# A half-width projection tile doubled to 128 columns, and moved to a bank of its own

## The chip, the cores and the metric

The kernel runs on one core of one Trainium2 chip. The metric is the device time of one launch in microseconds (us), as the median of several runs. The core has five engines, each with an instruction queue of its own that it works off in order: TensorE (PE in the profile, with its weight loads shown apart as PEld), VectorE (DVE), ScalarE (ACT), GpSimd (POOL) and SyncE (SP), which issues the transfers. PE writes to eight banks of PSUM, each with 128 partitions and 2 KB (512 fp32 values) in each partition; DVE and ACT read the banks.

A matmul on PE has a stationary operand, loaded first, of up to 128 rows (the dimension summed over) and up to 128 columns (the partitions of the output), and a moving operand. The profile writes the stationary operand as rows*columns, and then the moving one: `64*128 64x256` is a matmul with 64 rows and 128 columns in use, through which 256 columns of the moving operand pass.

## The reference

Four layers over a sequence of 2048 tokens of width 576, in bf16: attention, gated layer, attention, gated layer, all with a layer norm before and a residual sum after. Both attention layers use the same weights, as do both gated layers.

```python
def _A_ref(x, wqkv, wo):                    # 32 heads of 18, window of 8 with dilation 2
    qkv = (x @ wqkv).reshape(B, S, 3, H, Dh).transpose(2, 0, 3, 1, 4)
    q, k, v = qkv[0], qkv[1], qkv[2]
    ...
    attn = _softmax(logits, axis=-1)
    o = jnp.einsum("bhsw,bhswd->bhsd", attn, vg)
    return o.transpose(0, 2, 1, 3).reshape(B, S, D) @ wo

def _B_ref(x, w_gate, w_up, w_down):        # F = 4608
    h = (x @ w_gate) * (x @ w_up)
    return h @ w_down

x = x + _A_ref(_layernorm(x), wqkv, wo)
x = x + _B_ref(_layernorm(x), w_gate, w_up, w_down)
x = x + _A_ref(_layernorm(x), wqkv, wo)
x = x + _B_ref(_layernorm(x), w_gate, w_up, w_down)
```

## The kernel before

**Stages.** The tokens go through in 18 stages, each an attention part (`attention`) and a gated part (`glu`) over the same tokens of one layer pair. The first four stages have 128 tokens (`nst == 1`, `n = 128`), the other fourteen 256 (`nst == 2`, `n = 256`). While the gated part of one stage runs on PE, the attention part of a following one runs mostly on DVE, ACT and through transfers. Its few PE pieces, the projections among them, are put between the matmuls of the gated part. A planner (`Plan.run`) does that when the kernel is built, from estimated costs; what comes out is a fixed order of instructions on each engine.

**Banks.** The gated part and the projections share four banks, two called `pg` (gate) and two called `pu` (up). One `pg` and one `pu` together are a unit. A unit is given to one piece of work at a time. In the gated part PE fills `pg` and `pu` (L793 for the rows 0 to 511 of the width 576, L804 for the 64 rows left), ACT copies `pg` out (L815), and DVE multiplies `pu` into it (L816, output `h`). L832 and L834 then multiply `h` with the third weight into the banks `acc` and `acct`.

**Projections.** `project` takes two units, `ua` and `ub`, and makes three groups of matmuls, all by the helper `mm` at L469: `full` over the four blocks of 128 rows for the tiles of `ua`; then `tails`, over the last 64 rows, for the tiles of both units; then `full` for the tiles of `ub`. The 64 rows of the tails lie twice in SBUF, on partitions 0 to 63 and 64 to 127, and the list of tails says which half each of them uses. The profile shows two tails that stand next to each other, use different halves and write different banks, at the same time.

**Weights.** q, k and v have 576 columns each, 1728 together. In `wqkv` columns 0 to 511 are q, 512 to 1023 k, 1024 to 1535 v, and then come the remaining 64 of q (1536), of k (1600) and of v (1664). So there are thirteen tiles of 128 columns and a fourteenth of 64. A tile is written (bank, place in the bank, first column, columns), with bank 0 for `pg` and 1 for `pu`, and the place in steps of `n`. An entry of a list of tails is (half, unit, tile), with unit 0 for `ua`.

With 256 tokens there are two calls of `project`: "q" does q and k, 512 columns each, with four tiles in each unit. "v" has the tiles `ut` in `ua`, which are the rest of q with the rest of k, and the rest of v, and the tiles `uv` in `ub`, which are v's 512 columns. In "v" both tiles of `ua` lie in its `pg`, and its `pu` is not used. With 128 tokens there is one call, "a": `ua` has q and k, `ub` has v and `ut`, with `ut` in `pu`.

**Evictions.** `ev_t` (L550 for q, L522 or L520 for k and v) copies the three rests of 64 out of the unit to partitions 0 to 63 of `qT`, `kT` and `vT`. The rest of k comes from partitions 64 to 127 of its bank already before the change.

**Order.** PE, ACT and DVE each go through their fixed order. A piece of PE work that writes a bank waits until the engine that last read that bank is done.

## Time and profile before

| | |
|---|---|
| median of 3 runs | 1088.74 us (1088.43 to 1090.1) |
| profiled execution, first to last instruction (span) | 1085.9 us |
| DVE busy | 756.5 us (70%) |
| ACT busy | 369.4 us (34%) |
| DMA, HBM read and written | 125.11 MB and 10.88 MB |
| projections L469, matmuls into `pg` and into `pu` | 720 and 540 |

The median lies 2.8 us over the span: the span counts from the first to the last instruction, and the run's time takes in what lies around them. In a timeline a row is a stretch of like instructions: start, length, engine, line, operation, output and input, shapes, count, and where the engine had been idle before it, how long and what ended it. A matmul takes longer from start to end than the next one needs to follow it, since they are pipelined, so what a matmul costs is read from start to start.

### The profile page before, as it was taken

The numbers are of one execution on the slowest core, as the hardware profiler recorded it, in microseconds if no ns is written. First come the engines' busy times: TensorE is split into PE (matmuls) and PEld (weight loads), VectorE is DVE, ScalarE is ACT, GpSimd is POOL, SyncE is SP. The second block draws the span as 40 slices with busy tenths as digits, with TensorE's granted clock in tenths as the row PEclk, the third lists the DMA queues.
The fourth block names the chain that finished last, engine by engine and source line by source line (L and its number), as shares of the span: only waits on it lengthen the run. The fifth ranks groups of instructions, "written<-read, shape, count | busy, mean of one in ns | idle before, by whom it ended". The sixth has DMA issues, their size and how long they took to land.

```text
span 1085.9 us, 25407 instructions
## 1 busy us (share of the span) xinstructions
PE 1071.7 (99%) x10797; PEld 788.8 (73%) x10797; DVE 756.5 (70%) x1345; ACT 369.4 (34%) x756; POOL 8.7 (1%) x39
## 2 busy tenths in 40 slices
PE   8999999999999999999999999999999999999998
PEld 6787877777777777777777777777777777777775
DVE  7677987685959876685967769596876869472222
ACT  5544254332421444232133332333243332213121
POOL 3000000000000000000000000000000000000000
PEclk9999999999999999999999999999999999999999
DMA  9963764745253644435363634527263443534331
GB/s 275 343 191 101 208 167 114 183 81 160 78 149 109 145 134 106 114 98 164 104 172 108 150 104 117 136 77 169 83 162 91 116 126 99 156 110 119 97 112 55
DMA packets 155089, 146.16 MB, mean 135 GB/s; under 512 B 43104, under 2 KB 152672, under 8 KB 154976
## 3 DMA queue, kind: packets, MB, share of 16 engines
q1 hardware_dynamic: 154976, 144.55, 49.4%
q8 instruction: 84, 1.38, 0.5%
q14 instruction: 29, 0.24, 0.1%
HBM read 125.11 MB, written 10.88 MB: 125 GB/s over the span
## 4 chain that ended last, share of the span: by engine, by line
PE 95%; DVE 2%; DMA 1%; issue 1%; SPq 0%; ACT 0%; DVEq 0%; ACTq 0%
PE pg L793 24%; PE pu L793 23%; PE acc L832 23%; PE pg L804 7%; PE pg L469 7%; PE pu L469 4%; PE pa L746 4%; PE acct L834 3%; DMA wraw<-in_A_wqkv_dram 1%; DVE h L816 1%; DMA a_dram<-s 0%; SPq L257 0%; DVE prod L714 0%; DMA ab<-a_dram 0%; PE pa L680 0%
## 5 line engine op out<-in xcount | busy, mean ns | idle before, releaser
L816 DVE TENSOR_TENSOR h<-pu,g_sb 128x512 bf16<-128x512 f32 x288 | 196.5, 686 | 204.9 <-ACT g_sb L815 152.5
L815 ACT CAST g_sb<-pg 128x512 bf16<-128x512 f32 x288 | 168.3, 585 | 478.6 <-PE pu L804 393.1
L832 PE MATMUL acc<-wd,h 128*128 128x512 bf16 x1152 | 306.3, 380 | 0.0
L793 PE MATMUL pg<-xnT_B,wg 128*128 128x256 bf16 (+1 forms) x2592 | 300.8, 261 | 0.8 <-ACT xnT_B L431 0.8
L793 PE MATMUL pu<-xnT_B,wu 128*128 128x256 bf16 (+1 forms) x2592 | 299.3, 261 | 0.0
L793 PEld LDWEIGHTS <-wg 128*128 128x128 bf16 x2592 | 212.4, 98 | 61.3 <-issue 26.2
L793 PEld LDWEIGHTS <-wu 128*128 128x128 bf16 x2592 | 230.9, 98 | 23.3
L834 PE MATMUL acct<-wd,h 128*128 128x64 bf16 x1152 | 222.0, 193 | 0.0
L832 PEld LDWEIGHTS <-h 128*128 128x128 bf16 x1152 | 112.7, 98 | 118.0
L714 DVE TENSOR_TENSOR prod<-vT,ab 128x1280 bf16<-128x1280 bf16 (+1 forms) x127 | 93.1, 742 | 63.5 <-DMA ab<-a_dram 63.3
L469 PEld LDWEIGHTS <-wqkv 128*128 128x128 bf16 (+1 forms) x1260 | 97.0, 98 | 36.9 <-issue 18.9
L834 PEld LDWEIGHTS <-h 128*128 128x128 bf16 x1152 | 112.9, 98 | 2.2
L580 DVE TENSOR_TENSOR prod<-qT,kT 128x2560 bf16<-128x2560 bf16 (+1 forms) x72 | 95.6, 1332 | 1.0 <-ACT kT L522 0.4
L469 PE MATMUL pg<-xnT_A,wqkv 128*128 128x256 bf16 (+4 forms) x720 | 91.6, 262 | 1.9 <-issue 0.8
L731 DVE TENSOR_TENSOR oT<-oT,prod 128x1280 bf16<-128x1280 bf16 (+1 forms) x119 | 90.9, 764 | 3.1
L804 PE MATMUL pg<-xnT_B,wgu_t 64*128 64x256 bf16 (+1 forms) x648 | 88.0, 260 | 0.0
L804 PE MATMUL pu<-xnT_B,wgu_t 64*128 64x256 bf16 (+1 forms) x648 | 88.0, 260 | 0.0
L469 PE MATMUL pu<-xnT_A,wqkv 128*128 128x256 bf16 (+5 forms) x540 | 70.9, 261 | 2.7 <-DVE h L816 2.1
L804 PEld LDWEIGHTS <-wgu_t 64*128 64x128 bf16 x1296 | 47.0, 94 | 32.3 <-issue 27.8
L746 PE MATMUL pa<-wo_p,oT 128*128 128x288 bf16 x310 | 48.2, 286 | 0.1
L375 ACT ACTIVATE xn<-xf,nmr,rstd 128x576 bf16<-128x576 f32 x47 | 40.7, 866 | 8.8 <-DVE nmr L367 8.8
L584 DVE TENSOR_TENSOR prod<-prod 128x1024 bf16<-128x1024 bf16 (+1 forms) x64 | 41.1, 643 | 0.8
(117 smaller groups left out, 562.6 us busy)
## 6 DMA issues: line engine op xcount, KB each, us to landing
wd<-in_B_w_down_dram SPq DMA_DIRECT2D x324, 288.0 KB, 3.2
s_dram<-s SPq DMA_DIRECT2D x13, 512.0 KB, 3.7
prod<-s_dram SPq DMA_DIRECT2D x52, 128.0 KB, 2.9
ab<-a_dram SPq DMA_DIRECT2D x52, 128.0 KB, 2.7
wg<-in_B_w_gate_dram SPq DMA_DIRECT2D x6, 768.0 KB, 9.8
wu<-in_B_w_up_dram SPq DMA_DIRECT2D x6, 768.0 KB, 10.2
out_dram<-ob SPq DMA_DIRECT2D x8, 288.0 KB, 2.7
wraw<-in_A_wqkv_dram SPq DMA_DIRECT2D x4, 432.0 KB, 5.3
```

Of the source, the lines that this page charges most:

```text
L469: nc.tensor.matmul(bank(p_, u)[0:m, e * n:(e + 1) * n], lhsT=wqkv[r_, k, c0:c0 + m], rhs=xnT_A[r_, k, 0:n], start=start, stop=stop, skip_g ...
L580: nc.vector.tensor_tensor(late["prod"][p_ % 2][:, :, :, 0:n], q2, k2, op=ALU.mult)
L584: nc.vector.tensor_tensor(prod[:, :, 0:4:2, 0:n], prod[:, :, 0:4:2, 0:n], prod[:, :, 1:4:2, 0:n], op=ALU.add)
L714: nc.vector.tensor_tensor(js(dst), js(vT[:, :, o0:o0 + n]), abw, op=ALU.mult)
L731: op("DVE", 60 + 3 * n, lambda i_=i_: nc.vector.tensor_tensor(oT[:, :, 0:n], oT[:, :, 0:n], late["prod"][i_ % 2][:, 0, :, 0:n], op=ALU.add ...
L746: nc.tensor.matmul(b()[:, 0:HD], lhsT=oT[:, t, i * P:(i + 1) * P], rhs=wo_p[:, t, hh * HD:(hh + 1) * HD], start=(t == 0), stop=(t == KT - 1))
L793: nc.tensor.matmul(pt[:, e * n:(e + 1) * n], lhsT=w_[:, k, ft * P:(ft + 1) * P], rhs=xT[:, k, 0:n], start=(first and k == 0 and e == 0), s ...
L804: nc.tensor.matmul(ps[:, e * n:(e + 1) * n], lhsT=wgu_t[r_, ft * P:(ft + 1) * P], rhs=xT[r_, KF, 0:n], start=(first and e == 0), stop=not ...
L815: op("ACT", 590, lambda: nc.scalar.copy(g_sb[gs][:, 0:ul], pg[use["slot"]][:, 0:ul]), r=[f"wg_{j}_{u}"], w=[f"g{gs}"], prio=0)
L816: op("DVE", 690, lambda: nc.vector.tensor_tensor(hb[hs][:, 0:ul], pu[use["slot"]][:, 0:ul], g_sb[gs][:, 0:ul], op=ALU.mult), r=[f"wu_{j}_{ ...
L832: nc.tensor.matmul(acc[i][:], lhsT=lhs, rhs=wt[:, e % 2, 0:512], start=(ft == 0), stop=(ft == NFT - 1))
L834: nc.tensor.matmul(acct[:, i * TL:(i + 1) * TL], lhsT=lhs, rhs=wt[:, e % 2, 512:D], start=(ft == 0 and i == 0), stop=(ft == NFT - 1), skip ...
```

## The change

The rest of v becomes a tile of 128 columns: it begins at column 1600 instead of 1664, so it takes the 64 columns of k's rest, which are computed a second time and not read, and the 64 of v's. v's rest then stands on partitions 64 to 127 of the output, and the eviction reads it there. With 256 tokens the tile also moves from the second place in `pg` of `ua` to the first place in `pu` of `ua`, and the six tails of "v" are put in another order. With 128 tokens it stays in `pu` of `ub`, and the order stays. The number of matmuls is the same.

```diff
             uv = [(b_, e, 1024 + P * (2 * b_ + e), P) for b_ in range(2) for e in range(2)]
-            ut = [(0, 0, 1536, P), (0, 1, 1664, TL)]
-            tv = [(0, 1, uv[0]), (1, 1, uv[2]), (0, 1, uv[1]), (1, 0, ut[1]), (0, 0, ut[0]), (1, 1, uv[3])]
-            tb = 0
+            ut = [(0, 0, 1536, P), (1, 0, 1600, P)]
+            tv = [(0, 1, uv[0]), (1, 1, uv[2]), (0, 1, uv[1]), (1, 1, uv[3]), (0, 0, ut[0]), (1, 0, ut[1])]
+            tb, vb, vc = 0, 1, 0
         else:
             uq = [(b_, e, 512 * b_ + P * e, P) for b_ in range(2) for e in range(4)]
-            ut = [(1, 0, 1536, P), (1, 1, 1664, TL)]
+            ut = [(1, 0, 1536, P), (1, 1, 1600, P)]
             uv = [(0, e, 1024 + P * e, P) for e in range(4)]
-            tb = 1
+            tb, vb, vc = 1, 1, n
...
-                (390, lambda u, d: cp(d, vT[0:TL, KF, HALO:HALO + n], bank(tb, u)[0:TL, n:2 * n]), [f"v4{z}"], 0)]
+                (390, lambda u, d: cp(d, vT[0:TL, KF, HALO:HALO + n], bank(vb, u)[TL:P, vc:vc + n]), [f"v4{z}"], 0)]
```

## The prediction, made before the changed kernel ran

> **What bounds the kernel now.** I read the page first, then the clock, then what PE waited for.

> ```profile
> PE 1071.7 (99%) x10797; PEld 788.8 (73%) x10797; DVE 756.5 (70%) x1345; ACT 369.4 (34%) x756; POOL 8.7 (1%) x39
> ...
> PE 95%; DVE 2%; DMA 1%; issue 1%; SPq 0%; ACT 0%; DVEq 0%; ACTq 0%
> ```

> ```profile
> core 0: 1085.9 us, clock 0.999
> ```

> ```profile
> PE pu L469 <- DVE h L816: 2.1, 4, 0.8
> ...
> PE pg L469 <- issue: 0.8, 1, 0.8
> PE pg L793 <- ACT xnT_B L431: 0.8, 1, 0.8
> ```

> The first fence has the busy times and the chain that ended last by engine: PE is busy for 99% of the span and holds 95% of the chain. The granted clock is full. The third fence, PE's waits (total, times, longest), has as its largest entry 2.1 us in four waits, in the projections. So a matmul started earlier on PE ends the kernel earlier, unless one of these few waits takes it back. But busy PE is not PE at its rate, so I looked at how closely projection matmuls follow each other. First, which of them the change touches, from the groups by shape:

> ```profile
> L469 PE MATMUL pg<-xnT_A,wqkv 128*64 128x256 bf16 x56 | 8.7, 279 | 0.0
> ...
> L469 PE MATMUL pg<-xnT_A,wqkv 64*64 64x256 bf16 x14 | 4.1, 293 | 0.0
> ```

> That is four full ones and one tail in each of the 14 stages of 256 tokens. Now the timeline of PE in the last stage, first the projection "q", which has only tiles of 128 columns, then "v":

> ```profile
> 882.03 1.04 PE L469 MATMUL pg<-xnT_A,wqkv 128*128 128x256 bf16 x8
> 882.90 1.04 PE L469 MATMUL pu<-xnT_A,wqkv 128*128 128x256 bf16 x8
> 883.87 0.28 PE L469 MATMUL pg<-xnT_A,wqkv 64*128 64x256 bf16 x1
> 883.87 0.28 PE L469 MATMUL pu<-xnT_A,wqkv 64*128 64x256 bf16 x1
> 883.99 0.27 PE L469 MATMUL pg<-xnT_A,wqkv 64*128 64x256 bf16 x1
> ...
> 884.41 0.28 PE L469 MATMUL pg<-xnT_A,wqkv 128*128 128x256 bf16 x1
> ```

> ```profile
> 887.15 1.37 PE L469 MATMUL pg<-xnT_A,wqkv 128*128 128x256 bf16 x9
> 888.24 0.28 PE L469 MATMUL pu<-xnT_A,wqkv 64*128 64x256 bf16 x1
> 888.36 0.70 PE L469 MATMUL pg<-xnT_A,wqkv 64*128 64x256 bf16 x3
> 888.79 0.28 PE L469 MATMUL pu<-xnT_A,wqkv 64*128 64x256 bf16 x1
> 889.00 1.05 PE L469 MATMUL pg<-xnT_A,wqkv 128*128 128x256 bf16 x8
> ```

> In "q" eight full matmuls go from 882.03 to 882.90: 0.87 us, 0.11 each. The next eight, up to the first tail, take 0.97, so going from 128 rows to 64 costs 0.10. The eight tails start in pairs, two at the same instant (883.87), the next pair 0.12 later, and from the first tail to the next full matmul it is 0.54. In "v" eight full matmuls (the ninth of the first row is the first tail, beside the one at 888.24) take 1.09, and the six tails 0.76, though they are fewer than in "q".

> **The change part by part.** *Full matmuls of the fourteenth tile.* With 128 columns these eight are the like of the second eight of "q": 0.97 instead of 1.09, which saves 0.12. That is the price of changing from 128 columns to 64 in the middle.

> *Tails.* Three pairs would alternate halves and the banks `pg` and `pu` exactly as in "q". Four pairs take 0.54 there, and one pair less is one 256-column matmul less, 0.11, so 0.43 instead of 0.76: 0.33 saved. The cause is that the 64-column tail now is entered and left by a switch, and that it stands next to a tail of the same bank, so that it has no partner. Together 0.45 in an undisturbed stage.

> *Where "v" is cut up.* In two of the 14 stages the output projection L746 stands between the full matmuls and the tails, one of them here:

> ```profile
> 230.56 1.16 PE L469 MATMUL pg<-xnT_A,wqkv 128*128 128x256 bf16 x8
> 231.65 0.79 PE L746 MATMUL pa<-wo_p,oT 128*128 128x288 bf16 x5
> ```

> Eight matmuls again take 1.09, with only full-width work behind them, where the first row of "q" takes 0.87. Both the switch into 64 columns and the one out of it go away: 0.22, with the tails 0.55.

> *The stages with a wait.* The four waits of 2.1 us are first tails into `pu` of `ub`. The longest, on DVE and on PE:

> ```profile
> 826.76 0.68 DVE L816 TENSOR_TENSOR h<-pu,g_sb 128x512 bf16<-128x512 f32 x1
> 827.36 0.82 DVE L714 TENSOR_TENSOR prod<-vT,ab 128x1280 bf16<-128x1280 bf16 x1
> 828.09 0.69 DVE L816 TENSOR_TENSOR h<-pu,g_sb 128x512 bf16<-128x512 f32 x1
> ```

> ```profile
> 826.61 1.37 PE L469 MATMUL pg<-xnT_A,wqkv 128*128 128x256 bf16 x9
> 828.83 0.27 PE L469 MATMUL pu<-xnT_A,wqkv 64*128 64x256 bf16 x1 [0.85 <-DVE h L816]
> ...
> 829.49 0.50 PE L469 MATMUL pg<-xnT_A,wqkv 128*128 128x256 bf16 x3
> ```

> The second `h` ends at 828.78, and the wait at 828.83 whatever PE did before it, so the 0.12 is lost there. From then to the next full matmul it is 0.66, and would be 0.43: 0.23 saved.

> *The wait that the change adds.* `pu` of `ua`, so far unused in "v", is now written by the fifth matmul, 0.44 us after "v" starts (four times 0.11). Behind that matmul the whole of PE is queued. In the stage above the first `h` ends at 827.44, 0.83 after the start, so PE would stop for about 0.4 at the fifth matmul; but it stops until 828.83 anyway, so this costs nothing. In the last stage the bank was last read by a copy of k, and even the copy of the other unit, the later one, is over before "v" starts at 887.15:

> ```profile
> 886.37 0.59 ACT L522 CAST kT<-pu 128x512 bf16<-128x512 f32 x1 [0.28 <-PE pu L469]
> ```

> No price is taken for this wait. Its bound is in the rivals.

> *Weight loads.* 90 stationary operands (56 + 14 above, and 20 in the stages of 128 tokens) grow from 64 to 128 columns.

> ```profile
> L469 PEld LDWEIGHTS <-wqkv 64*128 64x128 bf16 x234 | 9.4, 94 | 12.8 <-issue 9.0 <-DVE wqkv L305 1.0 <-ACT wqkv L307 0.4
> L469 PEld LDWEIGHTS <-wqkv 128*64 128x64 bf16 x72 | 6.2, 109 | 3.7 <-issue 2.9
> ```

> A load of 128 columns takes 94 ns here and one of 64 takes 109, so the wider tile is no dearer to load; and the 0.11 spacing in "q" has such loads in it already. The cost is taken as 0. [...]

> *Evictions.* v's rest is read from partitions 64 to 127 of another bank, as k's rest is already. Same size, same place in ACT's order: 0. The instruction orders of DVE, POOL and SP are unchanged, no DMA moves, and ACT's differs only in the bank named.

> *Stages of 128 tokens.* The 72 loads above are 56 for the wide stages, and 16 for four of these. Tails of the fourth of them, at the place of the 64-column one:

> ```profile
> 65.24 0.22 PE L469 MATMUL pu<-xnT_A,wqkv 64*128 64x128 bf16 x1
> 65.30 0.22 PE L469 MATMUL pg<-xnT_A,wqkv 64*128 64x128 bf16 x1
> 65.44 0.24 PE L469 MATMUL pu<-xnT_A,wqkv 64*64 64x128 bf16 x1
> 65.61 1.28 PE L469 MATMUL pg<-xnT_A,wqkv 64*128 64x128 bf16 x18
> ```

> Paired with the one at 65.30, as those before it are, the tail lets the next start 0.06 later, at 65.36 instead of 65.61: 0.25. The switch into and out of the four full ones is the 0.22 of the cut-up stage. So 0.47 in the fourth stage. In the third there is a pause of 0.8 that ends by "issue" between its last tails (the waits above), of which I can't tell whether it moves along: 0.22 to 0.47, taken as 0.35. The first two lie before PE's wait for the first gated part (`xnT_B`, 0.8 above), which DVE and ACT work leads up to: 0 to 0.47 each, taken as 0.

> *Sum.* 14 wide stages: 8 x 0.45 = 3.60; 2 x 0.55 = 1.10; 4 x 0.23 = 0.92; together 5.62. Narrow: 0.47 + 0.35. In all 6.4 us off a span of 1085.9, which makes 1079.5. The runs' median lies 2.8 over the span, so 1088.74 - 6.4 = 1082.3.

> The bounds: nothing from the tails leaves 8 x 0.12 + 2 x 0.22 + 0.22 = 1.6 (1087.1). All four narrow stages in full (5.62 + 4 x 0.47) and no waits for `h` any more (2.1) would be 9.6 (1079.1).

> **The rivals.**
> *A. Only the full matmuls gain.* If the row change, and not the lack of a partner, made the tails slow, they stay at 0.76: 1087.1. For it: entering and leaving 64 rows stays. Against it: "q" has the same row change, and does four pairs in 0.54.

> *B. The new wait eats the gain.* Units come free in order, `ua` before `ub`. In the ten stages without a wait the first tail, 1.09 after the start, finds `ub` free, so the fifth matmul can wait for at most 1.09 - 0.44 = 0.65. Then the first tail comes 0.53 later than now and the tails still give back 0.33, so a stage loses 0.20; ten lose 2.0, the four others gain 0.92 and the narrow ones 0.8. Net 0.3 lost: 1089.0. For it: the first `h` at 827.44. Against it: that stage waits for `ub` anyway, and the copy of k at 886.96 was early.

> *C. Slower: wider loads come out on PE.* If the loads of the 64-column tiles took half of what those of 128 do, 47 of 94 ns, and PE stood still for the other 47 in each of 90 loads, this would cost 90 x 0.047 = 4.2, and if the pauses around the 64-column tile were load time too, nothing would be gained: 1093.0. [...] Against it: the rows of the loads, and the even spacing in "q". [...]

> *D. More than forecast.* The four waits for `h` also vanish, because transfers land earlier relative to PE: 2.1 more, 1080.2. Nothing in the change moves those transfers.

> **How the numbers follow.** Forecast 0.86, A 0.05, B 0.03, C 0.03, D 0.03. A difference of 0.2%, 2.2 us, is about what a measurement of this kernel can tell from no change. Forecast and D lie beyond it: faster 0.89. A and B lie within: same 0.08. C: slower 0.03. The predicted time is 1082.3. The range takes in D and the first two stages gaining in full on its low side, and half of the tails' gain missing (2.4) on its high side, with some room for the medians of three runs, which spread over 1.7 us: 1080.2 to 1085.4.

> **What would show it.** In the timeline of "v", eight full matmuls up to the first tail in 0.97, three pairs of tails starting at the same instants, 0.43 to the next full matmul, and so a start of the sixteen full ones 1.40 after that of "v" instead of 1.85. No group with 64 columns left. PE's waits for `h` still four, some a little longer, and one more at the fifth matmul around 827. The span near 1079.5, with PE's busy time down by as much. I am wrong if PE shows a wait at the fifth matmul in many stages, if the tails don't pair up, or if a wait elsewhere grows by several us.

## The result, and the profile after

| kernel | median | runs | ratio to the kernel before | 95% interval |
|---|---|---|---|---|
| before | 1088.1 us (1086.38 to 1090.1) | 6 | | |
| after | 1081.81 us (1079.86 to 1085.17) | 6 | 0.9943 | 0.9929 to 0.9958 |

The kernel became faster by 0.57%, 6.3 us; 6.4 were forecast. The profiled execution has a span of 1078.1 us. First the page of the kernel after, the engines' busy times and the chain by engine, then its clock:

```profile
PE 1063.8 (99%) x10797; PEld 787.7 (73%) x10797; DVE 755.1 (70%) x1345; ACT 369.4 (34%) x756; POOL 8.8 (1%) x39
...
PE 95%; DMA 2%; DVE 2%; SPq 1%; issue 1%; ACT 0%; DVEq 0%; ACTq 0%
```

```profile
core 0: 1078.1 us, clock 1.000
```

PE has the same 10797 matmuls, and its busy time fell from 1071.7 to 1063.8, by 7.9, as much as the span (7.8). The other engines' busy times moved by 1.4 us at most. So the time came out of PE's busy stretches, not out of its waits. PE is still 95% of the chain.

PE's waits in the kernel after (total in us, times, longest):

```profile
PE pu L469 <- DVE h L816: 2.1, 4, 0.5
...
PE pg L469 <- issue: 0.9, 1, 0.9
PE pg L793 <- ACT xnT_B L431: 0.8, 1, 0.8
```

The waits for `h` still come to 2.1 in four, the longest 0.5 instead of 0.8; the pause by "issue" and the wait for `xnT_B` are where they were. Now the timeline of PE in the last stage's "v", to be read beside the rows at 887.15 before:

```profile
879.65 0.60 PE L469 MATMUL pg<-xnT_A,wqkv 128*128 128x256 bf16 x4
880.09 0.60 PE L469 MATMUL pu<-xnT_A,wqkv 128*128 128x256 bf16 x4
880.62 0.28 PE L469 MATMUL pg<-xnT_A,wqkv 64*128 64x256 bf16 x1
880.62 0.28 PE L469 MATMUL pu<-xnT_A,wqkv 64*128 64x256 bf16 x1
880.74 0.27 PE L469 MATMUL pg<-xnT_A,wqkv 64*128 64x256 bf16 x1
880.74 0.27 PE L469 MATMUL pu<-xnT_A,wqkv 64*128 64x256 bf16 x1
880.85 0.27 PE L469 MATMUL pg<-xnT_A,wqkv 64*128 64x256 bf16 x1
880.85 0.27 PE L469 MATMUL pu<-xnT_A,wqkv 64*128 64x256 bf16 x1
881.05 1.05 PE L469 MATMUL pg<-xnT_A,wqkv 128*128 128x256 bf16 x8
```

From 879.65 to the first tail at 880.62 it is 0.97 (1.09 before), from there to the next full matmul at 881.05 it is 0.43 (0.76 before). The tails start two at a time, three times. In all eight stages that nothing disturbs, the two stretches are 970 and 434 ns, as they were 1087 and 760 in all eight before, to 1 ns (in three of the eight the output projection L746 follows the tails, and its first matmul ends the second stretch). Where the output projection L746 cuts "v" up, in the stage that stood at 230.56 before:

```profile
227.32 0.60 PE L469 MATMUL pg<-xnT_A,wqkv 128*128 128x256 bf16 x4
227.75 0.60 PE L469 MATMUL pu<-xnT_A,wqkv 128*128 128x256 bf16 x4
228.19 0.78 PE L746 MATMUL pa<-wo_p,oT 128*128 128x288 bf16 x5
```

The eight full ones now take 0.87 (1.09 before). Last, the groups of the kernel after by shape, weight loads and the full matmuls into `pg` (busy time, mean ns of one, idle time before them):

```profile
L469 PEld LDWEIGHTS <-wqkv 128*128 128x128 bf16 x1008 | 85.9, 98 | 19.6 <-issue 7.1 <-DVE wqkv L305 0.6 <-ACT wqkv L307 0.3
...
L469 PE MATMUL pg<-xnT_A,wqkv 128*128 128x256 bf16 x392 | 52.4, 273 | 0.0
```

No group with 64 columns is left, and a load of 128 columns takes 98 ns, where one of 64 took 109 before. All loads together (PEld) fell by 1.1 us.

### The profile page after: what moved, and what is told of

The parts are those of the page before. It is cut to its first block, busy times and chain, and to the rows that moved or that the text cites. A ratio compares the mean times of both kernels' runs of the same rounds, so it can differ in the third digit from the quotient of the medians.

```text
span 1078.1 us, 25413 instructions
## 1 busy us (share of the span) xinstructions
PE 1063.8 (99%) x10797; PEld 787.7 (73%) x10797; DVE 755.1 (70%) x1345; ACT 369.4 (34%) x756; POOL 8.8 (1%) x39
## 4 chain that ended last, share of the span: by engine, by line
PE 95%; DMA 2%; DVE 2%; SPq 1%; issue 1%; ACT 0%; DVEq 0%; ACTq 0%
PE pg L793 24%; PE pu L793 23%; PE acc L832 23%; PE pg L804 7%; PE pg L469 5%; PE pu L469 4%; PE pa L746 4%; PE acct L834 3%; DMA wraw<-in_A_wqkv_dram 1%; DMA a_dram<-s 1%; DMA ab<-a_dram 1%; DVE h L816 0%; SPq L257 0%; DVE prod L714 0%; PE pa L680 0%
## 5 line engine op out<-in xcount | busy, mean ns | idle before, releaser
L816 DVE TENSOR_TENSOR h<-pu,g_sb 128x512 bf16<-128x512 f32 x288 | 196.3, 686 | 200.8 <-ACT g_sb L815 149.6
L793 PE MATMUL pg<-xnT_B,wg 128*128 128x256 bf16 (+1 forms) x2592 | 300.8, 261 | 0.8 <-ACT xnT_B L431 0.8
L793 PE MATMUL pu<-xnT_B,wu 128*128 128x256 bf16 (+1 forms) x2592 | 299.3, 261 | 0.0
L793 PEld LDWEIGHTS <-wg 128*128 128x128 bf16 x2592 | 212.5, 98 | 61.2 <-issue 26.2
L793 PEld LDWEIGHTS <-wu 128*128 128x128 bf16 x2592 | 230.9, 98 | 23.3
L714 DVE TENSOR_TENSOR prod<-vT,ab 128x1280 bf16<-128x1280 bf16 (+1 forms) x127 | 92.9, 741 | 66.5 <-DMA ab<-a_dram 66.4
L469 PEld LDWEIGHTS <-wqkv 128*128 128x128 bf16 (+1 forms) x1260 | 95.4, 97 | 30.3 <-issue 16.1
L469 PE MATMUL pg<-xnT_A,wqkv 128*128 128x256 bf16 (+3 forms) x650 | 79.7, 260 | 1.5 <-issue 0.9
L469 PE MATMUL pu<-xnT_A,wqkv 128*128 128x256 bf16 (+3 forms) x610 | 76.5, 262 | 2.6 <-DVE h L816 2.1
L746 PE MATMUL pa<-wo_p,oT 128*128 128x288 bf16 x310 | 48.2, 286 | 0.1
```

The costliest lines, as they stand in the source:

```text
L469: nc.tensor.matmul(bank(p_, u)[0:m, e * n:(e + 1) * n], lhsT=wqkv[r_, k, c0:c0 + m], rhs=xnT_A[r_, k, 0:n], start=start, stop=stop, skip_g ...
L714: nc.vector.tensor_tensor(js(dst), js(vT[:, :, o0:o0 + n]), abw, op=ALU.mult)
L746: nc.tensor.matmul(b()[:, 0:HD], lhsT=oT[:, t, i * P:(i + 1) * P], rhs=wo_p[:, t, hh * HD:(hh + 1) * HD], start=(t == 0), stop=(t == KT - 1))
L793: nc.tensor.matmul(pt[:, e * n:(e + 1) * n], lhsT=w_[:, k, ft * P:(ft + 1) * P], rhs=xT[:, k, 0:n], start=(first and k == 0 and e == 0), s ...
L816: op("DVE", 690, lambda: nc.vector.tensor_tensor(hb[hs][:, 0:ul], pu[use["slot"]][:, 0:ul], g_sb[gs][:, 0:ul], op=ALU.mult), r=[f"wu_{j}_{ ...
```

## The experiments

Each run's ratio is to the kernel before on the same chip. Beside it stands, where it helps, the stretch of the trace from the first matmul of the first 256-token projection to the start of the kernel's last matmul, called the long stretch: 995.6 us before, 989.7 after. It leaves out the start, which varies for other reasons.

### Up bank and order, but 64 columns

The change moves a tile and pairs the tails, and also widens the tile. This does the first without the second, with 256 tokens only.

```diff
-            ut = [(0, 0, 1536, P), (0, 1, 1664, TL)]
-            tv = [(0, 1, uv[0]), (1, 1, uv[2]), (0, 1, uv[1]), (1, 0, ut[1]), (0, 0, ut[0]), (1, 1, uv[3])]
+            ut = [(0, 0, 1536, P), (1, 0, 1664, TL)]
+            tv = [(0, 1, uv[0]), (1, 1, uv[2]), (0, 1, uv[1]), (1, 1, uv[3]), (0, 0, ut[0]), (1, 0, ut[1])]
...
-                (390, lambda u, d: cp(d, vT[0:TL, KF, HALO:HALO + n], bank(tb, u)[0:TL, n:2 * n]), [f"v4{z}"], 0)]
+                (390, lambda u, d: cp(d, vT[0:TL, KF, HALO:HALO + n], bank(vb, u)[0:TL, vc:vc + n]), [f"v4{z}"], 0)]
```

> Only the bank and the order of the tails are changed in the 14 wide stages; the tile keeps its 64 columns, in all stages. Theory 'columns': the cost lies in going between 64 and 128 columns, whatever the bank. Then in the last wide stage eight full matmuls still take 1.09 us up to the first tail; two pairs of tails start together, the third pair does not (the 64-column tail starts 0.20 after its neighbour), and from the first tail to the next full matmul it is about 0.65 (two pairs 0.23, 0.20 into 64 columns, 0.22 out of it), so 1.74 from the start of "v" to the sixteen full ones (1.85 before, 1.40 with the change). The time is then about 1.4 us under before, 0.9987 of it. Rival 'partner': the tails were slow because neighbours shared a bank; then the tails take 0.43 here, 1.52 in all, and the time is about 4.5 us under before, 0.996.

Measured: 0.9981 (0.9968 to 0.9994), 1086.53 us in 12 runs; the long stretch 994.3, which is 1.3 shorter than before. The timeline of PE in the last "v":

```profile
885.42 0.60 PE L469 MATMUL pg<-xnT_A,wqkv 128*128 128x256 bf16 x4
885.95 0.62 PE L469 MATMUL pu<-xnT_A,wqkv 128*64 128x256 bf16 x4
886.51 0.28 PE L469 MATMUL pg<-xnT_A,wqkv 64*128 64x256 bf16 x1
...
886.74 0.27 PE L469 MATMUL pg<-xnT_A,wqkv 64*128 64x256 bf16 x1
886.94 0.29 PE L469 MATMUL pu<-xnT_A,wqkv 64*64 64x256 bf16 x1
887.16 0.28 PE L469 MATMUL pg<-xnT_A,wqkv 128*128 128x256 bf16 x1
```

Four full matmuls into `pg` go to 885.95, 0.53 instead of the 0.44 that the same four take in the kernel after: entering 64 columns costs 0.09, though the bank and the order are now those of the change. Together with the next four it is 1.09, as before. The last tail starts 0.20 after the one that should be its partner, with the other bank and the other half, and the next full matmul 0.22 after that. So the tails take 0.65. Of the 0.45 per stage, 0.11 belongs to bank and order, and 0.34 to the columns: 0.12 in the full matmuls, 0.22 in the tails.

### Only the stages of 256 tokens, and only those of 128

The first keeps the 64-column tile with 128 tokens, the second keeps everything as before with 256. Both diffs are against the kernel after; `vr`, set for each width of stage, is the first partition on which v's rest stands, 0 for 64 columns and 64 (`TL`) for 128.

```diff
             uq = [(b_, e, 512 * b_ + P * e, P) for b_ in range(2) for e in range(4)]
-            ut = [(1, 0, 1536, P), (1, 1, 1600, P)]
+            ut = [(1, 0, 1536, P), (1, 1, 1664, TL)]
...
-                (390, lambda u, d: cp(d, vT[0:TL, KF, HALO:HALO + n], bank(vb, u)[TL:P, vc:vc + n]), [f"v4{z}"], 0)]
+                (390, lambda u, d: cp(d, vT[0:TL, KF, HALO:HALO + n], bank(vb, u)[vr:vr + TL, vc:vc + n]), [f"v4{z}"], 0)]
```

```diff
-            ut = [(0, 0, 1536, P), (1, 0, 1600, P)]
-            tv = [(0, 1, uv[0]), (1, 1, uv[2]), (0, 1, uv[1]), (1, 1, uv[3]), (0, 0, ut[0]), (1, 0, ut[1])]
-            tb, vb, vc = 0, 1, 0
+            ut = [(0, 0, 1536, P), (0, 1, 1664, TL)]
+            tv = [(0, 1, uv[0]), (1, 1, uv[2]), (0, 1, uv[1]), (1, 0, ut[1]), (0, 0, ut[0]), (1, 1, uv[3])]
+            tb, vb, vc, vr = 0, 0, n, 0
...
-                (390, lambda u, d: cp(d, vT[0:TL, KF, HALO:HALO + n], bank(vb, u)[TL:P, vc:vc + n]), [f"v4{z}"], 0)]
+                (390, lambda u, d: cp(d, vT[0:TL, KF, HALO:HALO + n], bank(vb, u)[vr:vr + TL, vc:vc + n]), [f"v4{z}"], 0)]
```

> The change in the 14 stages of 256 tokens alone; the four stages of 128 tokens as before. The sum of the prediction has 5.6 us for these, 0.9948 of before, 1.40 us from the start of "v" to the sixteen full matmuls, and nothing gained up to the first gated part (33.65 us in the trace of before). If the first two stages, taken as 0 in the prediction, are worth the 1.0 us by which the changed kernel reached its first gated part earlier, this kernel reaches it as late as before; if that 1.0 was spread of the transfers at the start, it may reach it at any time within 1 us of both.

> The change in the four stages of 128 tokens alone; the 14 others as before. By the prediction 0.8 us under before (0.9993); if the first two stages count as the changed kernel's trace suggests, 1.9 us (0.9983), with the first gated part reached 1.0 us earlier than before. 1.85 us from the start of "v" to the sixteen full matmuls in the last stage in either case.

Measured: with 256 tokens alone 0.9938 (0.9926 to 0.995), 1081.56 us in 5 runs, the long stretch 5.7 shorter. With 128 tokens alone 1.0007 (0.9998 to 1.0015), 1089.06 us in 12 runs. The wide stages bring the whole gain, and the narrow ones, forecast at 0.8, brought none in these runs. The narrow stages' matmuls did become shorter. PE in the kernel with 128 tokens alone has a pause between the third stage's tails

```profile
43.49 1.21 PE L469 MATMUL pg<-xnT_A,wqkv 64*128 64x128 bf16 x17 [1.26 <-issue]
```

of 1.26, where it is 0.85 in the profiled execution of the kernel after. Something besides the tails varies there. And the long stretch, in which this kernel differs in nothing from the kernel before, is 0.8 longer in this trace: it has one wait for `h` more, in a "q", that the kernel before does not have.

```profile
385.76 1.03 PE L469 MATMUL pu<-xnT_A,wqkv 128*128 128x256 bf16 x8 [0.67 <-DVE h L816]
```

Either the narrow change moves such a conflict later on, or it is chance. The same kernel a second time, below, bears on that.

### One bank for both tiles

With 128 columns, but both tiles of `ua` in `pg`, and their tails last, in the same half. This takes away the write to `pu` of `ua`, so the new wait at the fifth matmul can't occur.

```diff
-            ut = [(0, 0, 1536, P), (1, 0, 1600, P)]
-            tv = [(0, 1, uv[0]), (1, 1, uv[2]), (0, 1, uv[1]), (1, 1, uv[3]), (0, 0, ut[0]), (1, 0, ut[1])]
-            tb, vb, vc = 0, 1, 0
+            ut = [(0, 0, 1536, P), (0, 1, 1600, P)]
+            tv = [(0, 1, uv[0]), (1, 1, uv[2]), (0, 1, uv[1]), (1, 1, uv[3]), (0, 0, ut[0]), (0, 0, ut[1])]
+            tb, vb, vc = 0, 0, n
```

> 128 columns in all stages, but in the wide ones the tile stays in the gate bank of its unit, at its second place, so the up bank is not written there and the wait at the fifth matmul cannot arise. [...] Theory 'columns': 0.97 up to the first tail, 0.54 from there to the next full matmul, 1.51 in all; the wait for h in the four stages ends as late as in the changed kernel; time 1.5 us above the changed kernel (14 x 0.11), 4.9 us under before (0.9955). Rival 'the new wait costs': if the wait at the fifth matmul costs the changed kernel something that the first tail's wait does not hide, the four stages are shorter here by that much, up to 0.4 us each, and the two kernels come out equal.

Measured: 0.9954 (0.9939 to 0.9969), 1083.55 us in 6 runs, the long stretch 3.4 shorter than before. PE in the last "v", the start of it and then the full matmuls behind its tails:

```profile
885.24 1.25 PE L469 MATMUL pg<-xnT_A,wqkv 128*128 128x256 bf16 x9
886.22 0.28 PE L469 MATMUL pu<-xnT_A,wqkv 64*128 64x256 bf16 x1
...
886.75 1.05 PE L469 MATMUL pg<-xnT_A,wqkv 128*128 128x256 bf16 x8
```

885.24 to the first tails is 0.97 again, and from 886.22 to 886.75 it is 0.54 (540 ns in all eight undisturbed stages, to 1 ns), 0.11 more than with pairs: a tail without a partner costs one more matmul of 256 columns. The stages that wait for `h` are not shorter without the fifth matmul's wait: the four together 10.06 us here, 9.18 in the kernel after, 10.24 before. Each has 0.11 more in its tails by design, and the waits for `h` were longer in this execution: 3.5 in five over the whole kernel, the longest 1.2. So this sum by itself neither shows nor rules out a cost of the fifth matmul's wait.

### The same kernel again, and the order of DVE

The first repeats the kernel with 128 tokens alone, for the question left open above. The second asks whether the remaining waits for `h` can be had. They arise where DVE's product of v (L714) stands in front of `h` and waits for its transfer, as in the kernel after on DVE, and on PE beside it:

```profile
818.76 0.82 DVE L714 TENSOR_TENSOR prod<-vT,ab 128x1280 bf16<-128x1280 bf16 x1 [8.24 <-DMA ab<-a_dram]
819.50 0.68 DVE L816 TENSOR_TENSOR h<-pu,g_sb 128x512 bf16<-128x512 f32 x1
820.10 0.81 DVE L714 TENSOR_TENSOR prod<-vT,ab 128x1280 bf16<-128x1280 bf16 x1
820.84 0.68 DVE L816 TENSOR_TENSOR h<-pu,g_sb 128x512 bf16<-128x512 f32 x1
```

```profile
819.67 0.60 PE L469 MATMUL pg<-xnT_A,wqkv 128*128 128x256 bf16 x4
820.24 0.60 PE L469 MATMUL pu<-xnT_A,wqkv 128*128 128x256 bf16 x4
820.77 0.28 PE L469 MATMUL pg<-xnT_A,wqkv 64*128 64x256 bf16 x1
821.57 0.27 PE L469 MATMUL pu<-xnT_A,wqkv 64*128 64x256 bf16 x1 [0.52 <-DVE h L816]
```

So the planner was told, from the kernel after, to place that product later in the stages from the seventh on:

```diff
-                   margin=0 if on_pe or i_ else 800 if j < 6 else 3500)
+                   margin=0 if on_pe or i_ else 800 if j < 6 else 5000)
```

> The kernel with the change in the four stages of 128 tokens alone, once more, because its first measurement (1.0007, interval 0.9998 to 1.0015) left out the 0.8 us that the prediction gave to these stages, while its trace shows them 0.77 us shorter from the first product to the end of the fourth projection, and 1.0 us of new waits for DVE and ACT in one later projection "q". Theory 'chance': that later wait belongs to transfers that land differently in each execution; then this trace has it at another place or not at all, and the two measurements together are between 0.999 and 1.0005. Rival 'tied': the shift by the narrow stages brings that wait about; then the same projection waits for 1.0 us again, and the time is again not under before.

> The changed kernel, and in the planner the first product with v of a stage (L714, the one that waits for the transfer of ab) is planned 1.5 us later from the seventh stage on (margin 5000 instead of 3500). Theory: the waits of PE for h, 2.1 us in four projections of the changed kernel, come from this product standing in front of two h in DVE's order while its transfer is still under way; planned later it stands behind them. Then PE's waits for h fall below 0.5 us in all, and the time is 1.5 to 2 us under the changed kernel, 0.9925 of before. Rival: the plan only moves the conflict, because every later piece of the stage moves too; then the waits for h are again about 2 us, at other places, and the time is that of the changed kernel, 0.9943.

Measured: 128 tokens alone, again, 0.9988 (0.9978 to 0.9998), 1086.74 us in 12 runs; its trace has no wait in that "q" (1.5 us in four for `h`), and its long stretch is 994.9, 0.7 shorter than before. The two runs of this kernel, 1.0007 and 0.9988, have intervals that only touch; their mean, 0.9998, is no change that these runs could tell. So the wait in "q" comes in one execution and not in the next. But it is not the chance of a single one: the repetition of the kernel after, further down, has the same wait in the same "q",

```profile
385.48 1.03 PE L469 MATMUL pu<-xnT_A,wqkv 128*128 128x256 bf16 x8 [0.67 <-DVE h L816]
```

and the kernels with one bank and with the narrow change in the third and fourth stage only have a shorter one there, 0.21 and 0.50. That is four of the eight traces with a narrow change and the old order of DVE, and none of the five without one. Whether the narrow change makes this wait likelier stays open.

The later product gave 0.9961 (0.9948 to 0.9974), 1084.47 us in 8 runs, above all others with the change in full. PE's waits there:

```profile
PE pu L469 <- DVE h L816: 3.7, 8, 0.5
```

Eight waits instead of four. The conflict of `h` and the product moved to other places and did not shrink, so the theory that the margin was too small falls. That it doubled is one trace: the trace with the narrow change in the third and fourth stage only, further down, has 3.0 in seven without this edit. Nor is the time all due to these waits, for this trace also lost 2.1 us at the start, in the way that the next section shows.

### What the narrow stages give back

The kernel after, the one with 256 tokens alone, and the kernel before, unchanged, together on one chip.

> The changed kernel once more, on the same chip as the kernel with the change in the wide stages alone, so that the two differ by the narrow stages only. The prediction gave those 0.8 us; the traces so far show the first product to the end of the fourth projection shorter by 0.7 to 1.2 us with them. If that reaches the end, this kernel is 0.8 us under the other; if the spread of the transfers at the start covers it, the two are within 0.5 us. From the end of the fourth projection to the last matmul the trace should again be about 5.6 us shorter than before (1013.8 us there), as in the first trace of this kernel (1007.9).

> The change in the 14 wide stages alone, once more, beside the changed kernel on one chip. 5.6 us under before, 0.9948. The trace from the end of the fourth projection to the last matmul as in its first one, 1008.1 us, within 1 us.

> The kernel before, for one more trace. If the first two microseconds of difference between the traces up to the end of the fourth projection are chance, this trace differs from the first one of the same kernel (67.4 us there) by about 1 us too; if they belong to the change, by less than 0.3. From there to the last matmul it is 1013.8 us, within 1 us.

Measured: after 0.9947 (0.9934 to 0.9961), 1082.68 us; 256 tokens alone 0.9948 (0.9935 to 0.996), 1082.62; the one run of the kernel before 1087.68. With or without the narrow change it is the same. The traces show one way in which the gain gets lost. This trace of the kernel after needs 19.04 us from the first matmul of L596 to the first gated part (L793), where its first one needed 16.96 and the kernel before 17.22. The windows of PE (us, its busy time and matmuls, granted clock, DMA share, GB/s), of the kernel after in this repetition:

```profile
16.00:18.00 2.00, 1.22 (x63) 1.00 0.80 222
18.00:20.00 2.00, 1.76 (x55) 0.77 1.06 398
20.00:22.00 2.00, 1.22 (x13) 0.50 1.11 339
```

The granted clock fell to a half from 19.1 to 25.9 us, while fillers, transposes and a projection ran. The first two rows of that projection, here and then in the first trace:

```profile
23.56 1.91 PE L469 MATMUL pg<-xnT_A,wqkv 128*128 128x128 bf16 x16
25.27 1.15 PE L469 MATMUL pu<-xnT_A,wqkv 128*128 128x128 bf16 x12
```

```profile
21.95 1.06 PE L469 MATMUL pg<-xnT_A,wqkv 128*128 128x128 bf16 x16
22.85 0.83 PE L469 MATMUL pu<-xnT_A,wqkv 128*128 128x128 bf16 x12
```

Sixteen matmuls take 1.71 from start to start at half clock and 0.90 at full clock. In all 2.1 us are lost, more than the narrow stages save. The traces with one bank and with the later product lost 1.9 and 2.1 in the same way (18.90 and 19.04 us). Why more often with the narrow change? The wait of PE before the first L596, in the kernel before and then the repetition of the kernel after:

```profile
16.43 0.33 PE L596 MATMUL acct<-prod,Esel 128*32 128x64 bf16 x20 [0.39 <-DVE prod L580]
```

```profile
16.35 0.33 PE L596 MATMUL acct<-prod,Esel 128*32 128x64 bf16 x20 [0.66 <-DVE prod L580]
```

The first stage's shorter tails only bring PE earlier to a wait for DVE, behind the same 21 filler matmuls (L759), and the idle time grows from 0.39 to 0.66 us. Over all runs of this study up to here and in the next experiment, a mean clock of 0.997 or less occurred in 19 of 55 runs of kernels with the change in the first stage (the one with more fillers left out), and in 11 of 88 of those without it, the kernel before among them. This is a rough sign: the mean also takes in the time behind the last matmul, where traces show up to 2.2 us of half clock that costs nothing. This was the theory to be tested next: idle time at the start costs clock.

### More fillers, and no change in the first two stages

The first leaves the change as it is and lets the planner put more fillers into PE's idle time at the start (227 of L759 instead of 127; 50 more were expected, 100 came out). Their product is not used. The second makes the narrow change in the third and fourth stage only; its eviction follows with `vr` as above. Beside them the kernel after, a third time.

```diff
-                    self.warm(min(44, int(max(0, t - clock["PE"] - 100) / 100)))
+                    self.warm(min(80, int(max(0, t - clock["PE"] - 100) / 60)))
```

```diff
-            ut = [(1, 0, 1536, P), (1, 1, 1600, P)]
+            ut = [(1, 0, 1536, P), (1, 1, 1664, TL) if j < 2 else (1, 1, 1600, P)]
```

> The changed kernel, with 50 more filler matmuls (L759, which write nothing that is read) in the first microseconds: the planner puts one for each 60 ns that it expects PE to be idle, instead of each 100 ns, and up to 80 in a row instead of 44. Theory 'clock': in the first stage the faster tails leave PE idle for 0.66 us instead of 0.39 before the first sums (L596), and in some executions the granted clock then falls to half for some 5 us, which costs 2 us up to the first gated part (19.0 instead of 17.0 us from the first L596, seen in three of six traces with the change in the narrow stages, in none of five without). With the gaps filled PE's clock stays at 1.00 from 14 to 30 us, the runs' mean clocks are all 0.998 or more, and no run lies over 1.5 us above the fastest; the median is 0.5 to 1 us under the changed kernel's on the same chip. Rival 'chance': the clock falls whatever PE does there; then as many runs as with the changed kernel have a mean clock of 0.997 or less, and the median is the same within 0.3 us.

> The change in the 14 wide stages and in the third and fourth of the narrow ones; the first two stages, whose PE work has gaps, as before the change. Theory 'clock': the idle time before the first L596 is 0.39 us again, so the clock falls no more often than with the wide stages alone (mean clock 0.997 or less in at most one run of five), and 0.5 to 0.8 us from the third and fourth stage come on top of what the wide stages give: 1080.9 to 1081.8, 0.994 of before. Rival 'nothing from the narrow stages': the same median as with the wide stages alone, 1081.6 to 1082.6.

> The changed kernel, as the control for the two others on the same chip. 1081.8 to 1082.7 as before; a mean clock of 0.997 or less in about a third of the runs by the theory 'clock' (in 16 of 49 so far with the change in the narrow stages, in about 8 of 73 without).

Measured on this chip:

| kernel | median | ratio | 95% interval | mean clock at most 0.997 |
|---|---|---|---|---|
| after, with more fillers | 1081.13 us | 0.9932 | 0.9919 to 0.9945 | 0 of 5 runs |
| narrow change in the third and fourth stage only | 1082.18 us | 0.9941 | 0.9929 to 0.9953 | 1 of 5 |
| after | 1084.0 us | 0.9951 | 0.9938 to 0.9965 | 3 of 6 |

The timeline of PE with more fillers, where the wait before the first L596 was:

```profile
13.89 2.13 PE L759 MATMUL pa<-ident 128*128 128x128 bf16 x35
16.11 0.33 PE L596 MATMUL acct<-prod,Esel 128*32 128x64 bf16 x20
```

and its windows:

```profile
16.00:18.00 2.00, 1.65 (x69) 1.00 0.90 326
...
22.00:24.00 2.00, 2.00 (x36) 1.00 1.06 365
```

The wait is filled, PE is busy for 1.65 of the 2 us from 16 on instead of the 1.22 of the repetition above, and the clock holds. It has the lowest median of all kernels here, 0.9932. The order of the three medians is what the theory asks for, but their intervals overlap, and with a chance of 19 in 55, five runs without a fall come up by luck once in 8 times (36/55 to the fifth power is 0.12). The kernel in the middle did not come out as the theory had it, at 1080.9 to 1081.8; 1082.18 is what its rival, that the narrow stages bring nothing, gave. The kernel after lies above the 1081.8 to 1082.7 expected, and the 2.9 us between it and the kernel with fillers are more than the 0.5 to 1 forecast.

Idle time can't be the whole of it either: the first trace of the kernel after had the same waits of PE around the first L596 as the repetition, and kept its clock. And without the narrow change in the first stages the clock can fall too, only earlier; in the repetition with 256 tokens alone:

```profile
14.00:16.00 2.00, 1.95 (x21) 0.63 0.58 107
16.00:18.00 2.00, 2.00 (x52) 0.51 0.84 266
```

There the stretch at half clock is mostly fillers and sums (L596), and from the first L596 to L793 it took 17.15 us, nothing lost. The trace with the narrow change in the third and fourth stage only is such a case too, and its mean clock of 0.997 is the one counted in the table.

The traces say more about which executions lose the clock. In all fourteen the granted clock changes only at whole multiples of 3.41 us from its first rise: the falls inside the kernel last 3.41 or 6.83 us, and the stretch at full clock lasts 1071.785 us in the first trace of the kernel after and 1078.612 in that of the kernel before, 314 and 316 times 3.41333. That rise, where the fillers' spacing goes from 107 to 56 ns, comes between 4.13 and 6.62 us after the first instruction (6.58 and 6.16 in these two), so these periods lie differently over the kernel in each execution. Count each matmul that starts in a period by its moving columns, times the share of the 128 rows and the share of the 128 columns of the stationary operand that it uses. Then the five periods at full clock ahead of a fall inside the kernel hold 2432 to 2976, and every other one at full clock, up to the last 10 us of the kernel, 3008 or more. The five, and two that kept the clock:

| execution | period, us | PE busy, us | columns so counted | granted clock after it |
|---|---|---|---|---|
| after, repetition | 15.68 to 19.10 | 2.09 | 2432 | half for 6.83 us |
| one bank for both tiles | 14.92 to 18.33 | 2.20 | 2624 | half for 6.83 us |
| later product | 16.31 to 19.72 | 2.21 | 2816 | half for 6.83 us |
| 256 tokens alone, repetition | 11.12 to 14.53 | 2.92 | 2848 | half for 3.41 us |
| third and fourth stage only | 11.45 to 14.86 | 2.94 | 2976 | half for 3.41 us |
| before, repetition | 14.98 to 18.39 | 2.40 | 3008 | full |
| after, first trace | 16.82 to 20.24 | 2.21 | 3328 | full |

So it is not idle time as such: PE's busy time doesn't tell these periods apart, the columns so counted do. The first row is 80 sums of L596, each 64 moving columns with 32 of 128 columns in use, which make 1280, and nine fillers of 128, which make 1152. With more fillers no stretch of 3.41 us between 6 and 60 us of that trace, wherever it begins, holds fewer than 3840, so no fall in five runs need not be luck. This count was found in the traces afterwards, and no run was made to test it.

## Why the prediction was right, point by point

**The sum of the wide stages** was forecast at 5.62. In the profiled executions the eight undisturbed stages gave 8 x (1.847 - 1.404) = 3.54, for 3.60; the two that are cut up 2.565 - 2.016 = 0.55 each, as said; and the four that wait went from 10.24 to 9.18 together, 1.06 for 0.92. That is 5.70, and the long stretch became 5.92 shorter. With 256 tokens alone it was 5.68. Over all seven traces that have this part of the change and the old order of DVE (three of the kernel after, two with 256 tokens alone, and the two of the last experiment) the stretch is 990.5 on the mean, against 995.7 in two of the kernel before: 5.2 less. The spread between them (989.7 to 991.8) is of the size of the waits for `h`, which differ by several tenths from one execution to the next.

**Both pieces of it** hold: 0.12 for the full matmuls is the price of the columns, measured apart by the tile in its own bank with 64 columns. Of the tails' 0.33, put down to the switch and to the missing partner together, the bank and order alone give 0.11, which is the partner, and the columns 0.22. The two add up: the kernel with one bank has the columns without the partner, and its tails go from 0.76 to 0.54, again 0.22. Each part can be had alone, the whole 0.45 only with both.

**Rival A**, only the full matmuls gain, falls with the 0.43. Four pairs in "q" were the right measure for three in "v".

**Rival B**, the new wait at the fifth matmul: it is there, but in three stages only, all of which wait for `ub` anyway. In the rows at 819.67 the fifth matmul starts 0.57 after the first instead of 0.44, so 0.13 of wait, and the first tail into `pu` then still waits 0.52 for the second `h`. The other two are 0.04 and 0.28. The eleven other stages have none. In all three the first tail waits 0.52 more behind it, for the other unit, so the fifth matmul's wait lies inside a wait that PE has anyway. The kernel that can't have it had longer waits for `h` in its one trace, and settles nothing here.

**Rival C**, dearer loads, falls with the row of loads: 98 ns for 128 columns. That a load of 64 columns takes half of one of 128, 47 of 94 ns, is shown by no run; it took 109. **Rival D**, the waits for `h` vanish: they stayed at 2.1, and in the attempt to move them away they were 3.7.

**The narrow stages**, forecast at 0.82, are the term that was mis-sized. On PE's work the size was right or low: where the clock held, the stretch from the first L596 to the first L793 became 0.15 to 0.27 shorter, which was taken as 0, and the one from there to the first wide projection 0.5 to 0.9 (51.0 to 51.4 us instead of 51.9), together 0.8 to 1.2, with the pause that I could not place making up part of the spread. What the prediction left out is the other side of "the first two lie before PE's wait, taken as 0": a shorter piece in front of a wait means a longer idle time. Here this went with a granted clock at half in three of the seven traces with the change in the first stage (fillers left out), which lost 1.9 to 2.1 us by it, and with a lower mean clock in about a third of the runs. The longer idle time is part of what makes a period poor in matmul columns, but by the table above not the whole. A second thing that can take the gain back is the wait for `h` in a "q", 0.2 to 0.7 us in four of eight traces. On the medians the narrow part then came to nothing: 1082.68 with it and 1082.62 without, on one chip.

**Why the total still fits.** The profiled execution gained 7.8, not 6.4, but it is the fastest of the six runs (1079.86) and had a full clock: 5.9 in the long stretch, and 1.9 ahead of it, 0.72 of them before the first L596 (16.43 to 15.71), which no step of the forecast covers, 0.27 and 0.9 in the narrow stages. The 0.72 is spread of the start: over the fourteen traces, with the change and without, the first L596 comes between 15.7 and 17.1. The same spread is in the 2.8 us between median and span before: in every run with both on record the time is only 1.7 to 1.9 over its own span, so the execution profiled before was about a microsecond faster than that median. The runs gained 6.3. With 256 tokens alone the runs gained 6.6 and 5.95, beside 5.7 and 5.5 in the long stretch of their traces; a difference of half to one microsecond is less than the intervals of some 1.3 us either way can tell. So the wide stages carry the result, and that it came within 0.1 us of the forecast, with the narrow stages' 0.82 gone on the medians, is luck within that spread.

**What stays open**: how often the clock falls in each kernel, since the count by periods was not put to the test; whether the narrow change makes the wait in "q" likelier; what the pause in the third stage is; and whether more fillers would also help the kernel without the narrow change, which was not tried.

## What to carry to other kernels

On a PE-bound kernel, look for the one tile of another width: fourteen times four matmuls and a tail of 64 columns, with the partner that the tail lost, cost 5.7 us here, and computing 64 columns twice was free: a full matmul of 64 columns took no less than one of 128 (279 and 273 ns on the mean), and neither did its load (109 and 98). Read PE by starts, not by busy share: 99% busy held these pauses. And when a piece in front of a wait gets shorter, ask what keeps PE at work in the idle time that it leaves; with more fillers this kernel kept its clock in all five runs, though its median is not clear of the others.

## What the runs showed of the hardware

Entering 64 columns from 128, with all 128 rows, cost 0.09 us (885.42 to 885.95 against 0.44), as much as going from 128 rows to 64 does (0.10). A load of 64 columns took longer than one of 128, 109 against 98 ns. A 64-column tail between tails of 128 columns lost its partner although half and bank differed: 0.20 in, 0.22 out.

The granted clock fell to a half (0.50) with 0.66 us, before the first L596, as the longest idle time of PE in the 5 us ahead of it. In another execution of the same kernel it stayed full with the same wait of 0.66, here on PE in the first trace of the kernel after:

```profile
15.71 0.33 PE L596 MATMUL acct<-prod,Esel 128*32 128x64 bf16 x20 [0.66 <-DVE prod L580]
```
